# Where the last three batches' softmax steps stand: eb6 behind gp7, pd6 behind pe7, later pL5 and pe5, batch 4's maximum ahead of its clip

## The chip, the core and the metric

The kernel runs on one core of a Trainium2 chip. Its engines work side by side, each in the order of its own list: TensorE (PE) multiplies, VectorE (DVE), ScalarE (ACT) and GpSimd (POOL) work element by element, SyncE (SP) issues DMA transfers, and ScalarE issues some too. The metric is the time of one execution on the device, in microseconds; less is better.

## What is computed

```python
X = np.fft.rfft(x, axis=1)                       # x: 8 batches x 2496 x 256
Yr = Xr @ w_r - Xi @ w_i + b_r
Yi = Xr @ w_i + Xi @ w_r + b_i
Y = softshrink(Yr, 0.01) + 1j * softshrink(Yi, 0.01)
x = np.fft.irfft(Y, n=2496, axis=1).reshape(19968, 256)

logits = x @ phi                                 # phi: 256 x 32
d = exp(logits - logits.max(0)); d /= d.sum(0) + 1e-9
slot_input = d.T @ x                             # 32 slots, 4 for each of 8 experts
slot_out[e] = relu(slot_input[e] @ w1[e]) @ w2[e]
c = exp(logits - logits.max(1)); c /= c.sum(1) + 1e-9
out = c @ slot_out
```

The softmax `d` runs over all 19968 tokens, so its maximum and its sum are carried from batch to batch; the softmax `c` runs over the 32 slots of each token.

## The kernel before

A transform of length 2496 = 39 x 64 is done in two stages by matrix products. Each batch has five steps of four frequencies (`NGRP` = 5). In a step PE makes `px` (second stage), `pk` and `py` (the product with the weights, each operand split into a high and a low part), the other engines make `xth`, `xtl`, `xsm`, `xs` (operands) and `ut`, `rt` (softshrink), and PE makes `pq` (logits in the frequency domain, copied as `lg`). `pt` are transposes of `rt` into `T`.

When a batch's five steps are through, its softmax chain follows (`c_stages(b)`, for the last batch `last_chain`), interleaved with the steps of the next batches. Its pieces, with the batch number behind the name:

- `pg`: inverse of the 64-point stage; `g_sb` is written to DRAM as `gd` (320 KB) and read back transposed as `gp` (four loads, 330 KB together). In the last chain the write is cut in three (192, 64 and 64 KB) and issued by ScalarE.
- `pL`: logits, in two halves `pL_0`, `pL_1`. DVE reduces each half to a maximum `mx`, ScalarE copies it to `L`. In batches 0 to 5 `pL` has high and low parts (`chpL`, `clpL`) and both halves use the one buffer of the PSUM tag `ps`.
- `pm`, `mall`, `dg`, `pb`: running maximum, transposed and spread over the partitions.
- `ee`: exponential; `pe`: first stage of it (in batches 0 to 5 from `chpe`, `clpe`); `ea`, written to DRAM as `ed` and read back as `eb` (two loads, 320 KB together, in rows of 128 bytes).
- `pd`: second stage, `dd`; `pr`: the sum of `dd` times `T`; `acc`: running sum, updated from `pr` by `slots_out`.

After batch 7's `pr` come `psl` (slot inputs), `hps` and `po` (the two products of the experts, whose weights `w` were loaded on the way), `prep`, and the output: `pc` (transposes of `c`), `pq`, `ost` and 41 writes.

The order on every engine is set by the program's own order. Each piece is a generator that yields a time in planned microseconds; a heap runs whichever comes first, and what is recorded then is issued in that order. The numbers are in `PLAN`: `late` has one list for each of the batches 4, 5 and 6 (`pL`, `pe`, `pd`, `pr` are offsets from the batch's start `t0`), `T_` the numbers of the last part, whose origin is `TB`. In `last_chain`, transposes wait in `fills` under a key and `fill(...)` lets them go where PE would otherwise wait; (2, 0) to (4, 1) are batch 6's, (7, 0) belongs to batch 7's first step. `halves` runs one product in two halves: it yields, issues the matmuls, yields `de` later and lets the result be copied (`evac`). All matmuls are recorded in line 244, transposes in 641, elementwise operations in 183, SyncE's DMAs in 238, ScalarE's in 241.

Of the kernel before, what the change touches and what calls it, by code (L numbers as in the profile page):

```python
# [17 lines left out]
B, N, D = 8, 2496, 256  # L18
# [34 lines left out]
def _constants():  # L53
# [133 lines left out]
def fourier_soft_moe_kernel(ctx: ExitStack, tc: tile.TileContext, t: dict, out: bass.AP):  # L187
# [19 lines left out]
    def psum(tag, name):  # L207
        return pp.tile([128, 512], F32, tag=tag, name=name, bufs=psum_bufs[tag])
# [8 lines left out]
    x = t["x"]  # L217
# [6 lines left out]
    V, A, P = (_InOrder(tc, e) for e in (nc.vector, nc.scalar, nc.gpsimd))  # L224
# [12 lines left out]
    def sp(**kw):  # L237
        tc.keep_in_program_order(nc.sync.dma_start(**kw))
# [4 lines left out]
    def mm(**kw):  # L243
        tc.keep_in_program_order(nc.tensor.matmul(**kw))  # L244
# [61 lines left out]
    xs = wtile([128, 6 * KS], F32R, "xs", "xs")  # L306
# [9 lines left out]
    ident, sgn, suni, sinv, dsc, dmask = (cols[k] for k in ("ident", "sgn", "suni", "sinv", "dsc", "dmask"))  # L316
    f1, m2 = cols["f1"][:P1], cols["m2"][:Q1]
# [369 lines left out]
        else:  # L687
            cins[b] = [cb[:, :GX, :], cb[:, GX:, :]]

    def halves(n, t0, times, out, const, fr, src, evac, de=0.25):  # L690
        xs = []
        xw = 352 if n in ("m2", "f1") else 320
        low = lambda x, xh, xl: V.tensor_tensor(out=xl, in0=x, in1=xh.bitcast(F32), op=ALU.subtract)
        late = n == "m2"
        for h in range(2 * fr[n]):
            dh = (PLAN["clm"] if late else PLAN["cl"][1]) * h
            yield t0 + times[0] - PLAN["cl"][0] + dh
            x = src(h)
            m, w = x.shape[0], x.shape[1] * x.shape[2]
            xh, xl = (  # L700
                wtile([128, 352], F32R, z, f"{z}{out[0]}_{h}")[:m, :w].rearrange("p (k s) -> p k s", s=S)
                for z in ("ch", "cl")
            )
            A.copy(out=xh, in_=x)
            xs.append((xh, xl))
            yield t0 + times[0] - PLAN["cl"][0] + dh + PLAN["cl"][2]
            low(x, xh, xl)
        for h in range(2):
            yield t0 + times[h]
            ps = psum("pl" if n == "suni" and h and not fr[n] else "ps", f"{out[0]}_{h}")  # L710
            if fr[n]:
                ch, cl = const_hl[n]
                for i, (w_, x_) in enumerate(((ch, xs[h][0]), (cl, xs[h][0]), (ch, xs[h][1]))):
                    mm(out=out[1](ps)[:, :xw], lhsT=w_, rhs=x_, start=i == 0, stop=i == 2)
            else:
                mm(out=out[1](ps)[:, :xw], lhsT=const, rhs=src(h), start=True, stop=True)
            yield t0 + times[h] + de
            evac(h, out[1](ps))

    def c_stages(b):  # L720
        ct_ = "ps"
        K_ = dict(PLAN, **PLAN["late"].get(str(b), {}))
        t0 = 20 * b + 20 + LAG
# [3 lines left out]
        fr = K_["fr"]  # L727
# [10 lines left out]
        for r in range(R):  # L738
# [14 lines left out]
        def logits_out(h, ps):  # L753
# [19 lines left out]
        ps = psum(ct_, f"pm{b}")  # L773
# [11 lines left out]
        else:  # L785
# [3 lines left out]
        ps = psum(ct_, f"pb{b}")  # L789
# [4 lines left out]
            out=ee, in0=L, in1=ps[:P1, :32].unsqueeze(1).broadcast_to([P1, G, S]), op=ALU.subtract  # L794
# [11 lines left out]
        yield t0 + K_["pe"][1] + 0.35  # L806
        ed = dr.tile([2 * K1, NP, S], F32, tag="ed", name=f"ed{b}")
        sp(out=ed.rearrange("k (r g) s -> (k r) g s", r=R), in_=ea)
        yield t0 + K_["pe"][1] + 0.9
        eb = wtile([128, K1, S], F32, "gp", f"eb{b}")  # L810
        for c in range(2):
            sp(out=eb[c * 64 : c * 64 + 64], in_=ed[c * K1 : c * K1 + K1, :N2].rearrange("k n s -> n k s"))
# [5 lines left out]
                out=dd[:, h * 10 : h * 10 + 10, :],  # L818
# [13 lines left out]

    prs = {}
# [181 lines left out]
    T_ = PLAN["T_"]  # L1015
# [5 lines left out]
    def last_chain():  # L1021
        b = B - 1
        for (k0, k1), tk in zip(((0, 12), (12, 16), (16, 20)), T_["pg"]):
            ks = slice(k0, k1)
            n = (k1 - k0) * S
# [4 lines left out]
            ps = psum("pf", f"pg{b}_{k0}")  # L1030
# [5 lines left out]
        for r in range(R):  # L1036
# [67 lines left out]
        eb = wtile([128, K1, S], F32, "gp", f"eb{b}")  # L1104
# [183 lines left out]
    for j in range(NBLK):  # L1288
# [81 lines left out]
```

## Time and profile before

| | |
|---|---|
| median of 3 runs | 523.17 us (522.37 to 523.2) |
| profiled execution | 522.57 us |
| its span | 520.8 us |
| PE busy | 502.7 us (97%) |
| DVE, ACT, POOL busy | 405.6, 312.8, 295.5 us |
| granted PE clock, mean | 0.993 |

A row of a timeline gives the start, the duration, the engine, the source line and the operation with its output and input; in brackets stands how long the engine was idle before it, and what released it. Neighbouring matmuls overlap: one is listed with some 0.28 us, and the next starts 0.12 us after it, so for PE the step from start to start counts. A clock of 1.00 is 2.4 GHz. Engines other than PE have idle time nearly everywhere, and it costs nothing unless PE waits for them.

### The profile page before, as it was taken

Reading aid. Unit: us, or ns where it says so; the run is one execution under the profiler, and the core shown is the slowest. Engines: PE = TensorE matmul, PEld = TensorE weight load, DVE = VectorE, ACT = ScalarE, POOL = GpSimd, SP = SyncE. Lnnn points to the kernel's source line nnn. Section 1 sums busy time; section 2 is a strip of 40 time slices with the busy share of each in tenths; the row PEclk is TensorE's granted clock in tenths of the full one; section 3 lists DMA queues with packets and bytes.
Section 4 is the critical chain, followed back from the end, with each engine's and each line's share of the span. In section 5 each row is a group of like instructions: output and inputs, shape, how many; then the busy total and the mean of one; then the engine's idle time right before and its main releaser. Section 6 shows DMA issues by size and latency. Waiting matters only on the chain.

```text
span 520.8 us, 12050 instructions
## 1 busy us (share of the span) xinstructions
PE 502.7 (97%) x4473; PEld 440.9 (85%) x4473; DVE 405.6 (78%) x778; ACT 312.8 (60%) x704; POOL 295.5 (57%) x278
## 2 busy tenths in 40 slices
PE   8999999999999999999999999999999999999991
PEld 7888899999899999999998998889899877458880
DVE  3796787799968898889888988897798856257771
ACT  2776576768676766676667666654543436148761
POOL 1486687768676757675767577776466303054210
PEclk9999999999999999999999999999999999999997
DMA  8555456665765657565756576676655577979998
GB/s 295 220 185 185 136 183 227 168 238 130 280 166 188 162 200 210 174 162 193 210 176 164 188 212 211 165 274 209 235 143 158 180 174 213 409 249 406 400 409 333
DMA packets 90146, 114.85 MB, mean 221 GB/s; under 512 B 46478, under 2 KB 65868, under 8 KB 90088
## 3 DMA queue, kind: packets, MB, share of 16 engines
q1 hardware_dynamic: 89377, 112.90, 66.0%
q10 hardware_dynamic: 711, 1.19, 0.7%
q8 instruction: 35, 0.57, 0.4%
q14 instruction: 23, 0.19, 0.1%
HBM read 66.72 MB, written 47.34 MB: 219 GB/s over the span
## 4 chain that ended last, share of the span: by engine, by line
PE 85%; DVE 5%; DMA 4%; ACT 2%; issue 1%; SPq 1%; DVEq 0%; ACTq 0%
PE py L244 20%; PE px L244 13%; PE pk L244 10%; PE pq L244 10%; PE pa L244 9%; PE pt L641 6%; PE pr L244 3%; PE pe L244 2%; PE q L244 2%; PE pc L1169 2%; PE pL L244 2%; PE pg L244 1%; PE hps L244 1%; PE po L244 1%; DMA gp<-gd 1%; DMA out<-ost 1%
## 5 line engine op out<-in xcount | busy, mean ns | idle before, releaser
L183 POOL TENSOR_TENSOR xs<-xsm,xs 128x256 fp32r<-128x256 f32 x77 | 63.2, 821 | 97.7 <-DVE xs L183 67.5
L183 POOL TENSOR_TENSOR rt<-ut,rt 128x512 f32<-128x512 f32 x79 | 105.0, 1329 | 14.8 <-DVE rt L183 13.4
L183 POOL TENSOR_TENSOR xl<-xr,xh 117x512 fp32r<-117x512 f32 x72 | 97.7, 1358 | 15.2 <-ACT xh L183 15.2
L244 PE MATMUL px<-smov,ap 128*128 128x128 f32 x640 | 85.1, 276 | 0.4 <-DVE ap L183 0.3
L244 PEld LDWEIGHTS px<-smov,ap 128*128 128x128 f32 x640 | 80.3, 191 | 5.1 <-DVE ap L183 0.6
L183 DVE SCALAR_TENSOR_TENSOR ut<-py,pk,k 128x256 f32<-128x256 f32 x160 | 69.5, 475 | 11.4 <-PE py L244 11.1
L183 ACT CAST xth<-px 128x512 fp32r<-128x512 f32 x80 | 46.9, 587 | 45.4 <-PE px L244 23.2
L183 ACT COPY ast<-pa 128x512 f32<-128x512 f32 x75 | 44.2, 590 | 45.7 <-PE pa L244 45.7
L183 DVE TENSOR_TENSOR xtl<-px,xth 128x512 fp32r<-128x512 f32 x80 | 54.7, 684 | 20.3 <-ACT xsm L183 20.3
L244 PE MATMUL pk<-xs,w_rh 128*128 128x256 f32 (+1 forms) x320 | 66.1, 290 | 0.0
L183 DVE TENSOR_SCALAR rt<-ut 128x512 f32<-128x512 f32 x69 | 63.8, 924 | 0.5
L244 PE MATMUL py<-xth,nwsh 128*128 128x256 f32 (+1 forms) x160 | 53.4, 334 | 0.1
L244 PEld LDWEIGHTS pk<-xs,w_rh 128*128 128x128 f32 x320 | 51.8, 189 | 0.6 <-DVE xs L183 0.3
L183 ACT CAST xh<-xr 117x512 fp32r<-117x512 f32 x75 | 47.5, 636 | 1.0 <-DMA xr<-in_x 1.0
L641 PE MATMUL pt<-pk,rt 128*128 128x128 f32 x320 | 45.2, 274 | 1.2 <-DVE ap L183 1.1
L183 ACT COPY T<-pt 128x512 f32<-128x512 f32 x67 | 39.8, 600 | 8.9 <-PE pt L641 7.3
L244 PE MATMUL py<-xth,wdh 128*128 128x256 f32 (+1 forms) x160 | 44.8, 280 | 0.0
L244 PE MATMUL py<-xtl,wdh 128*128 128x256 f32 (+1 forms) x160 | 44.6, 278 | 0.0
L244 PE MATMUL py<-xtl,nwsh 128*128 128x256 f32 (+1 forms) x160 | 44.5, 278 | 0.0
L244 PE MATMUL py<-xth,nwsl 128*128 128x256 f32 (+1 forms) x160 | 44.5, 278 | 0.0
L244 PE MATMUL py<-xth,wdl 128*128 128x256 f32 (+1 forms) x160 | 44.4, 278 | 0.0
L244 PE MATMUL pk<-xs,w_rl 128*128 128x256 f32 (+1 forms) x160 | 44.4, 278 | 0.0
(196 smaller groups left out, 1192.3 us busy)
## 6 DMA issues: line engine op xcount, KB each, us to landing
out<-ost SPq DMA_DIRECT2D x37, 512.0 KB
xr<-in_x SPq DMA_DIRECT2D x35, 512.0 KB
ap<-adr SPq DMA_DIRECT2D x70, 256.0 KB
adr<-ast SPq DMA_DIRECT2D x21, 768.0 KB
w<-in_moe_w SPq DMA_DIRECT2D x25, 512.0 KB
w<-in_moe_w SPq DMA_DIRECT2D x12, 256.0 KB
x<-in_x SPq DMA_DIRECT2D x11, 256.0 KB
eb<-ed SPq DMA_DIRECT2D x16, 160.0 KB
```

The source lines that it names most:

```text
L183: return lambda *a, **k: self.tc.keep_in_program_order(f(*a, **k))
L244: tc.keep_in_program_order(nc.tensor.matmul(**kw))
L641: tc.keep_in_program_order(nc.tensor.transpose(out=out, in_=in_, identity=identity))
L1169: nc.tensor.transpose(out=pc[:, i * P1 : (i + 1) * P1], in_=chls[b][x][:, 2 * (r + i) : 2 * (r + i) + 2].rearrange("p g h s -> p (g h s)") ...
```

## The change

No arithmetic is added or removed; every instruction of before is still there. What moves:

- Batch 6's `eb` loads are planned at 21.015 instead of 0.9 behind `pe`, and stand on SyncE's list behind the four `gp7` loads.
- Batch 6's `pd` is planned at 30.6 instead of 20.25, and stands behind `pe7`; its two halves use the tags `pl` and `pf` (`pt` in the list), and its results are read at once.
- The second half of batch 7's first transposes (`pt7_0_1`) becomes a filler, key (7, 1), and stands ahead of `pe7`; step 1 of batch 7 (`pt7_1`) moves ahead of `pr6`.
- The last three transposes `pc0_8` of batch 0's `c` stand behind `pd7`.
- Batch 5: `pL` from 6.5, 7.2 to 7.02, 8.05 and `pe` from 11.35, 12.35 to 12.05, 12.6.
- Batch 4: the first half's `evac` 0.05 behind its matmuls instead of 0.25, which puts its maximum ahead of the clip `rt`.
- `slots_out` of batches 0 to 4 is 0.65 behind the last `pr` instead of 0.2: `acc` stands behind the next `xtl`, `xsm`, `xs` on DVE.

```diff
-'6': {... 'pd': [20.25, 20.62], ...}
+'6': {... 'eb': 21.015, 'pt': ['pl', 'pf'], 'de': 0.005, 'pd': [30.6, 30.61], ...}
-'5': {... 'pL': [6.5, 7.2], ... 'pe': [11.35, 12.35], ...}
+'5': {... 'pL': [7.02, 8.05], ... 'pe': [12.05, 12.6], ...}
+'4': {'me': [0.05, 0.25], ...}
...
-            ps = psum("pl" if n == "suni" and h and not fr[n] else "ps", f"{out[0]}_{h}")
+            ps = psum(tags[h] if tags else "ps", f"{out[0]}_{h}")
...
-            yield t0 + times[h] + de
+            yield t0 + times[h] + de[h]
...
-        yield t0 + K_["pe"][1] + 0.9
+        yield t0 + K_.get("eb", K_["pe"][1] + 0.9)
...
-        yield tk + (0.01 if b >= B - 3 else 0.2)
+        yield tk + (0.01 if b >= B - 3 else 0.65)
         slots_out(b)
...
-            key = (g_, h) if b_ == B - 2 and g_ >= 2 else (7, 0) if (b_, g_, h) == (B - 1, 0, 0) else None
+            key = (g_, h) if b_ == B - 2 and g_ >= 2 else (7, h) if (b_, g_) == (B - 1, 0) else None
...
-        fill((4, 1), (7, 0))
+        fill((4, 1), (7, 0), (7, 1))
...
+    at(10.9, fill, (7, 1))
...
-    for t_, f_, *a_ in ((T_["cl"], c_load, 0), (11.9, c_prep, 0), *((12.45 + 0.01 * i, c_trans, 0, i, V if i == 4 else A) for i in (0, 4, 8))):
+    for t_, f_, *a_ in ((T_["cl"], c_load, 0), (11.9, c_prep, 0), *((t_, c_trans, 0, i, V if i == 4 else A) for t_, i in ((12.45, 0), (12.49, 4), (19.5, 8)))):
```

SyncE's list at the start of the last chain, before (`ed6` is the write that `eb6` reads back, `w14` are expert weights, `cin0` is batch 0's `c`):

```order
L238 DMA ed6_6240<-ea6_6161 120x704
L238 DMA w14_0_6242<-in_moe_w1 128x512
L238 DMA w14_1_6243<-in_moe_w1 128x512
L238 DMA eb6_6256<-ed6_6240 64x20x32 x2
L238 DMA gp7_6412<-gd7_6263 40x22x32 x2
L238 DMA gp7_6412<-gd7_6263 40x20x32
L238 DMA gp7_6412<-gd7_6263 40x2x32
L238 DMA cin0_6419<-c_dr0_131 117x512
```

The two `eb6` loads are issued there ahead of `gp7`. SyncE's list at the same place now:

```order
L238 DMA ed6_6240<-ea6_6161 120x704
L238 DMA w14_0_6242<-in_moe_w1 128x512
L238 DMA w14_1_6243<-in_moe_w1 128x512
L238 DMA gp7_6402<-gd7_6259 40x22x32 x2
L238 DMA gp7_6402<-gd7_6259 40x20x32
L238 DMA gp7_6402<-gd7_6259 40x2x32
L238 DMA eb6_6409<-ed6_6240 64x20x32 x2
L238 DMA cin0_6413<-c_dr0_131 117x512
```

The two `eb6` loads have moved behind the four `gp7` loads and stand right ahead of `cin0`.

PE's list at the end of `pr5`, some way ahead of `pL7`, before (`pk0` holds the identity matrix):

```order
L244 MATMUL pr5_6355<-T5_3_5520,dd5_5714 32x256 x4
L244 MATMUL pr5_6355<-T5_4_5521,dd5_5714 32x256 x4
L244 MATMUL pd6_0_6380<-eb6_6256,pk1_120 128x320
L641 MATMUL pt6_0_0_6384<-pk0_119,rt6_0_0_5079 128x128
L641 MATMUL pt6_0_0_6384<-pk0_119,rt6_0_1_5151 128x128
```

`pd6_0` stands right behind `pr5` there, and `pd6_1` eight transposes further on. PE's list around `pe7` now:

```order
L641 MATMUL pt7_0_1_6482<-pk0_119,rt7_0_0_5774 128x128
L641 MATMUL pt7_0_1_6482<-pk0_119,rt7_0_1_5822 128x128
L244 MATMUL pe7_0_6496<-ee7_6487,pk1_120 120x352
L244 MATMUL pe7_1_6499<-ee7_6487,pk1_120 120x352
L244 MATMUL pd6_0_6511<-eb6_6409,pk1_120 128x320
L244 MATMUL pd6_1_6514<-eb6_6409,pk1_120 128x320
L641 MATMUL pt7_1_0_6519<-pk0_119,rt7_1_0_5874 128x128
```

Both halves of `pd6` have left the transposes ahead of `pL7` and stand behind `pe7`, and the four transposes of `pt7_0_1` stand ahead of it.

DVE's list around batch 5's maximum, before:

```order
L183 TENSOR_SCALAR rt6_2_1_5437<-ut6_2_1_5434 128x512
L183 TENSOR_REDUCE mx5_5355<-pL5_0_5471 117x32
L183 TENSOR_TENSOR xtl6_4_0_5467<-px6_4_0_5447,xth6_4_0_5466 128x512
L183 TENSOR_TENSOR xsm6_4_0_5468<-px6_4_0_5447,xsm6_4_0_5468 128x256
L183 CAST xs_118<-xsm6_4_0_5468 128x256
L183 TENSOR_REDUCE mx5_5355<-pL5_1_5498 117x32
L183 SCALAR_TENSOR_TENSOR ut6_3_0_5509<-py6_3_0_5480,pk0_119,k16_3_5478 128x4x64 x2
L183 TENSOR_REDUCE mall_126<-pm5_5507 128x1
```

Each reduction `mx5` is done there as soon as its half of `pL5` is. DVE's list at the same place now:

```order
L183 TENSOR_SCALAR rt6_2_1_5437<-ut6_2_1_5434 128x512
L183 TENSOR_TENSOR xtl6_4_0_5466<-px6_4_0_5440,xth6_4_0_5465 128x512
L183 TENSOR_TENSOR xsm6_4_0_5467<-px6_4_0_5440,xsm6_4_0_5467 128x256
L183 CAST xs_118<-xsm6_4_0_5467 128x256
L183 TENSOR_REDUCE mx5_5355<-pL5_0_5488 117x32
L183 SCALAR_TENSOR_TENSOR ut6_3_0_5498<-py6_3_0_5474,pk0_119,k16_3_5472 128x4x64 x2
L183 TENSOR_REDUCE mx5_5355<-pL5_1_5516 117x32
L183 TENSOR_REDUCE mall_126<-pm5_5525 128x1
```

The first reduction `mx5` from `pL5_0` has moved behind `xtl6_4_0`, `xsm6_4_0` and `xs`, and the second behind `ut6_3_0`.

## Rows read from the trace of the kernel before

**Rows 1.** Page, part 4, whole span: chain that ended last, by engine.

```profile
PE 85%; DVE 5%; DMA 4%; ACT 2%; issue 1%; SPq 1%; DVEq 0%; ACTq 0%
```

**Rows 2.** Timeline (start us, us, engine, operation [idle before]), batch 4's maximum: DVE, then PE.

```profile
312.40 0.41 DVE L183 TENSOR_SCALAR rt<-ut 128x512 f32<-128x512 f32 x1
...
312.84 0.28 PE L244 MATMUL py<-xtl,wdh 128*128 128x256 f32 x1
...
313.30 0.42 PE L244 MATMUL pL<-chpL,m2h 120*117 120x352 f32 x1 [0.18 <-DVE mx L183]
```

**Rows 3.** Timeline, batch 5's maximum: PE, then DVE.

```profile
360.36 0.32 PE L244 MATMUL pL<-chpL,m2l 120*117 120x352 f32 x1
360.82 0.42 PE L244 MATMUL pL<-clpL,m2h 120*117 120x352 f32 x1
...
361.13 0.42 DVE L183 TENSOR_SCALAR rt<-ut 128x512 f32<-128x512 f32 x1
...
362.21 0.68 DVE L183 TENSOR_TENSOR xtl<-px,xth 128x512 fp32r<-128x512 f32 x1
...
363.46 0.55 DVE L183 TENSOR_REDUCE mx<-pL 117x32 f32<-117x384 f32 x1
```

**Rows 4.** Timeline, batch 5's exponential: GpSimd, DVE, PE.

```profile
370.09 1.29 POOL L183 TENSOR_TENSOR rt<-ut,rt 128x512 f32<-128x512 f32 x1 [0.36 <-DVE rt L183]
...
370.57 1.19 DVE L183 TENSOR_TENSOR clpe<-ee,chpe 117x352 fp32r<-117x352 f32 x1 [0.56 <-ACT chpe L183]
...
372.94 0.52 DVE L183 TENSOR_TENSOR clpe<-ee,chpe 117x352 fp32r<-117x352 f32 x1
...
370.95 0.32 PE L244 MATMUL pe<-chpe,f1l 117*120 117x352 f32 x1
371.82 0.42 PE L244 MATMUL pe<-clpe,f1h 117*120 117x352 f32 x1 [0.55 <-DVE clpe L183]
```

**Rows 5.** Timeline of SyncE's queue, last chain: issue times of loads.

```profile
417.69 2.22 SPq L238 DMA_DIRECT2D eb<-ed  x2
...
423.37 2.71 SPq L238 DMA_DIRECT2D gp<-gd  x4
...
438.00 1.42 SPq L238 DMA_DIRECT2D eb<-ed  x2
```

**Rows 6.** Chain in order of time (start us, us, what): two writes of gd.

```profile
301.96 2.41 DMA gd<-g_sb
...
420.16 3.19 DMA gd<-g_sb
```

**Rows 7.** Windows: engines' busy us, PEclk, DMA share, GB/s, in the last chain.

```profile
419.50:422.00 2.50, 2.47 (x23) 2.23 (x21) 2.26 (x4) 1.48 (x4) 0.00 (x0) 1.00 0.90 164
424.60:427.00 2.40, 2.40 (x19) 1.95 (x16) 1.67 (x3) 0.58 (x1) 0.00 (x0) 1.00 0.81 127
427.60:434.00 6.40, 5.87 (x40) 4.71 (x39) 5.05 (x12) 3.66 (x9) 0.00 (x0) 1.00 0.79 283
436.80:442.50 5.70, 5.41 (x47) 4.94 (x47) 4.58 (x7) 3.84 (x8) 4.93 (x9) 1.00 0.91 219
```

**Rows 8.** Timeline of PE in the last chain.

```profile
426.06 0.70 PE L244 MATMUL pd<-eb,pk 128*128 128x320 f32 x2
426.61 1.06 PE L641 MATMUL pt<-pk,rt 128*128 128x128 f32 x8
...
427.90 1.41 PE L244 MATMUL pL<-gp,pk 120*117 120x352 f32 x4 [0.23 <-DMA gp<-gd]
...
431.60 1.07 PE L641 MATMUL pt<-pk,rt 128*128 128x128 f32 x8
...
432.97 1.45 PE L244 MATMUL pe<-ee,pk 117*120 117x352 f32 x4 [0.30 <-ACT ee L183]
...
440.69 1.02 PE L1169 MATMUL pc<-pk,chl 117*128 117x117 f32 x8
...
442.56 1.32 PE L244 MATMUL pd<-eb,pk 128*128 128x320 f32 x4
```

More of the change, by code (lines that the diff above doesn't have):

```diff
@@ L152 @@
     "to": 0.7,
-    "late": {'6': {'cms': [11.5, 19.69, 854.1, 854.2, 854.2, 854.2], 'pd': [20.25, 20.62], 'pr': [31.55, 31.6, 31.65, 31.7, 31.75], 'pL': [6.05, 6.5], 'pm': 8.05, 'mo': 0.1, 'pb': 9.05, 'eo': 0.4, 'pe': [11.1, 11.5], 'pg': [0.875, 1.275], 'fr': {'sinv': 0, 'm2': 0, 'f1': 0, 'suni': 0}}, '5': {'cms': [14.3, 14.8, 15.6, 20.0, 20.8, 21.5], 'pg': [1.1, 1.8], 'pL': [6.5, 7.2], 'pm': 8.52, 'de': 0.68, 'mo': 0.1, 'pb': 9.05, 'eo': 0.1, 'fr': {'sinv': 1, 'm2': 1, 'f1': 1, 'suni': 0}, 'pe': [11.35, 12.35], 'pd': [18.9, 19.3], 'pr': [40.2, 40.21, 40.22, 40.23, 40.24]}, '4': {'pr': [18.4, 20.49, 24.49, 28.49, 32.49]}},
@@ L154 @@
-    "T_": {'wl': [[-45, 'r'], [-44, 'r'], [-43, 'r'], [-31.0, 't'], [-30.7, 't'], [-29.4, 't'], [-27.6, 't'], [-27.8, 't'], [-11, 'a'], [-10.3, 'a'], [-9.6, 'a'], [-9.45, 'sm'], [-9.4, 'xs'], [-8.3, 'x'], [-8.1, 'x'], [1.06, 'x'], [1.07, 'h'], [1.08, 'h'], [13.55, 'h'], [13.55, 'h'], [13.55, 'h'], [13.55, 'h'], [13.55, 'h'], [13.61, 't'], [13.61, 't'], [13.61, 't'], [13.61, 't'], [13.61, 't'], [13.7, 'T'], [13.7, 'T'], [13.7, 'T']], 'cl': 1.02, 'cp': 46.5, 'ct': 46.6, 'du': [[-4.5, 0], [-2.4, 0], [1.2, 0]], 'd1': [5, 2, 4, 0, 0, 0], 'cm': [19.9, 19.91, 19.92, 25, 25.1, 25.2], 'cm7': [0.1, 0.12, 0.3, 0.4, 1, 1], 'ye': 0.2, 'te': [[5.6, 0.2], [5.5, 0.4]], 'pg': [-7, -3.25, -0.35], 'yt': 0.5, 'wr': -30.6, 'tp': [0, 0.9, 1.05, 0.3], 'tt': [[-3.6, -0.3, -0.25, -0.2, -6.5], [0.6, 0.7, 0, 0, 0], [12, 12.1, 12.2, 12.3, 12.4]], 'tg': {(5, 4): ('ps', 'pl'), (5, 0): ('pl', 'ps')}, 'eg': {(5, 4, 1): 'A', (6, 2, 1): 'A', (6, 4, 0): 'V', (6, 4, 1): 'A'}, 'z': 13.55, 'th': [0.1, 0.12], 'tl': [0.2, 0.25]},
+    "late": {'6': {'cms': [11.5, 19.69, 854.1, 854.2, 854.2, 854.2], 'eb': 21.015, 'pt': ['pl', 'pf'], 'de': 0.005, 'pd': [30.6, 30.61], 'pr': [31.55, 31.6, 31.65, 31.7, 31.75], 'pL': [6.05, 6.5], 'pm': 8.05, 'mo': 0.1, 'pb': 9.05, 'eo': 0.4, 'pe': [11.1, 11.5], 'pg': [0.875, 1.275], 'fr': {'sinv': 0, 'm2': 0, 'f1': 0, 'suni': 0}}, '5': {'cms': [14.3, 14.8, 15.6, 20.0, 20.8, 21.5], 'pg': [1.1, 1.8], 'pL': [7.02, 8.05], 'pm': 8.52, 'de': 0.68, 'mo': 0.1, 'pb': 9.05, 'eo': 0.1, 'fr': {'sinv': 1, 'm2': 1, 'f1': 1, 'suni': 0}, 'pe': [12.05, 12.6], 'pd': [18.9, 19.3], 'pr': [40.2, 40.21, 40.22, 40.23, 40.24]}, '4': {'me': [0.05, 0.25], 'pr': [18.4, 20.49, 24.49, 28.49, 32.49]}},
@@ new lines @@
+    "T_": {'wl': [[-45, 'r'], [-44, 'r'], [-43, 'r'], [-31.0, 't'], [-30.7, 't'], [-29.4, 't'], [-27.6, 't'], [-27.8, 't'], [-11, 'a'], [-10.3, 'a'], [-9.6, 'a'], [-9.45, 'sm'], [-9.4, 'xs'], [-8.3, 'x'], [-8.1, 'x'], [1.06, 'x'], [1.07, 'h'], [1.08, 'h'], [13.55, 'h'], [13.55, 'h'], [13.55, 'h'], [13.55, 'h'], [13.55, 'h'], [13.61, 't'], [13.61, 't'], [13.61, 't'], [13.61, 't'], [13.61, 't'], [13.7, 'T'], [13.7, 'T'], [13.7, 'T']], 'cl': 1.02, 'cp': 46.5, 'ct': 46.6, 'du': [[-4.5, 0], [-2.4, 0], [1.2, 0]], 'd1': [5, 2, 4, 0, 0, 0], 'cm': [19.9, 19.91, 19.92, 25, 25.1, 25.2], 'cm7': [0.1, 0.12, 0.3, 0.4, 1, 1], 'ye': 0.2, 'te': [[5.6, 0.2], [5.5, 0.4]], 'pg': [-7, -3.25, -0.35], 'yt': 0.5, 'wr': -30.6, 'tp': [0, 0.9, 1.05, 0.3], 'tt': [[-3.6, -0.3, -0.25, -0.2, -6.5], [0.6, 0.7, 0, 0, 0], [12, 11.45, 12.2, 12.3, 12.4]], 'tg': {(7, 0): ('pt', 'ps'), (5, 4): ('ps', 'pl'), (5, 0): ('pl', 'ps')}, 'eg': {(5, 4, 1): 'A', (6, 2, 1): 'A', (6, 4, 0): 'V', (6, 4, 1): 'A'}, 'z': 13.55, 'th': [0.1, 0.12], 'tl': [0.2, 0.25]},
@@ L688, in c_comb, with halves @@
             cins[b] = [cb[:, :GX, :], cb[:, GX:, :]]
-    def halves(n, t0, times, out, const, fr, src, evac, de=0.25):
+    def halves(n, t0, times, out, const, fr, src, evac, de=(0.25, 0.25), tags=None):
         xs = []
@@ L767, in c_stages @@
             logits_out,
+            K_.get("me", [0.25] * 2),
         )
@@ L822, in c_stages @@
             ),
-            K_.get("de", 0.25),
+            [K_.get("de", 0.25)] * 2,
+            K_.get("pt", None if fr["suni"] else ("ps", "pl")),
         )
```

## The prediction

> **What bounds the kernel now.** I read the chain of waits first: TensorE (PE) holds 85% of the span, so a microsecond counts only if a wait on PE goes away [rows 1]. Then I read PE's timeline for places where the step from one start to the next is longer than the same step elsewhere. Between 60 and 420 us there are few, and this change touches two of them: batch 4's maximum at 313 us [rows 2], and batch 5's maximum and exponential at 361 and 371 us [rows 3, 4]. The rest is the last chain, from 424 us on [rows 8]; there DMA round trips stand between PE's pieces [rows 5 to 7]. After the last `pr` the kernel runs on from what that chain gives it (slots, two matrix products, output), and none of that is edited, so I carry a shift there to the end one to one.
>
> **Batch 4: maximum ahead of clip.** VectorE (DVE) did a clip (0.41 us from 312.40) before the reduction that frees `pL4`'s only PSUM buffer; PE's next `pL` started 0.46 us after the `py` ahead of it, where such a step is 0.12, and it waited for that reduction [rows 2]. With the reduction first, it ends some 0.4 us sooner and the wait is gone: 0.34 of the step, and a little of the slow first `pL` (0.42 us): **0.4 us gained** (bounds 0 and 0.45). The clip is late by half a microsecond for a subtraction that nobody waits for here.
>
> **Batches 0 to 4: the accumulator update moves behind three operations.** Order on DVE only; I find no PE wait there that it ends, except beside batch 5's exponential, counted below. Zero.
>
> **Batch 5: pL behind the next py, pe behind the next px.** Before, PE lost 0.30 us inside `pL5_0`: the step from 360.36 to 360.82 is 0.46 us, where 352 columns at the 0.12 of 256 make 0.16 [rows 3]. Now a whole `py` (1.4 us) stands ahead, so that wait goes. But `pL5_1` now follows after one `px` (0.8 us), and its buffer is free only after the first reduction, which DVE does behind the trio `xtl`, `xsm`, `xs`. The trio starts when the clip ends (361.13 + 0.42 = 361.55) and lasts 1.25 us (362.21 to 363.46) [rows 3]; a reduction of 0.5 follows, to 363.3. PE gets there at 360.2 (`pL5_0`'s begin before, a step ahead of 360.36) + 1.4 + 0.5 + 0.8 = 362.9. So a new wait of 0.4 to 0.5 takes the place of the old: **0.1 lost**, and up to 0.5 if ScalarE, which then copies the second half, the maxima and the next `xth` in a row, brings `dg` late for `pb`. The exponential: PE's step from 370.95 to 371.82 is 0.87 us, 0.7 too long, for `clpe`, which took 1.19 us because it ran beside a GpSimd subtraction until 371.38; the other `clpe` took 0.52 [rows 4]. Now `clpe` comes behind the trio, at 372.0 to 372.5, while PE, with `px` first, is ready for it at about 372.1. A wait of 0.4 to 0.5 stays where 0.7 was: **0.2 gained** (bounds: 0.7, if `clpe` is in time, and 0.6 lost, if GpSimd's next subtraction is first and holds it for 0.7 as before). Batch 5 together: zero, from 0.6 gained to 1.1 lost.
>
> **The last chain up to pL7.** SyncE loaded `eb6` from 417.69 to 419.91, in packets so small that the 16 DMA engines were 0.90 busy with 164 GB/s until 422 [rows 5, 7]. ScalarE's last write of `gd7` went out at 420.16 in the middle of it and landed 3.19 us later; the same tensor of an earlier batch, all 320 KB at once, landed in 2.41 [rows 6], and this piece is 64 KB. With `eb6` behind `gp7` the write is alone. I take 2.0 us for it (under 2.41, the nearest row, since a fifth of the bytes move; 3.19 if nothing changes): 1.2 us sooner, bounds 0 and 1.45, past which PE is not ready for `pL7`. SyncE then issues `gp7` (four loads from 423.37 [rows 5]) 1.2 us sooner, unhindered as now; `eb6` follows in the same queue and does not overtake it. PE must be ready by then: `pd6`, two matmul groups of 0.55 (426.06 to 426.61) to 0.7 us each (its listed time), is gone from there, so the last transposes (426.61, 1.06 us) end at 426.4 and not 427.7 [rows 8]. `pL7` starts at 426.7 instead of 427.90.
>
> **From pL7 to pe7.** 5.07 us (427.90 to 432.97), a chain through DVE, PE and ScalarE with PE's fillers measured to it [rows 8]. The four transposes of `pt7_0_1` that move ahead of `pe7` take half of 0.9 us (431.60, eight of them) and fit in the 0.47 us that PE stood idle for `ee` [rows 8]. No change in length: `pe7` at 431.8.
>
> **From pe7 to pd7.** Before, 9.59 us (432.97 to 442.56). Out go 0.45 for `pt7_0_1` and the third group of `pc0`: eight transposes from 440.69 end at 441.6, so `pc0_8` with its wait took 0.97. In comes `pd6`, 1.2. That makes 9.4, so PE is at `pd7` at 441.2, and 0.2 goes back because `pc0_8` now stands between `pd7` and `pr7`, where PE waited for DVE only in part. `pr6` waits for `dd6`, but 0.9 us of `pt7_1` lie between, enough for DVE's 0.5 us a half. The other condition is `eb7`: its loads were issued at 438.00 for 1.42 us [rows 5], and `pd7` shows that it was there by 442.56; 1.2 sooner that is 441.3 at the latest, so it may cost 0.1. **The last chain gains 1.1 us**, bounds 0 (`gd7` as late as before) and 1.5.
>
> **Sum.** 0.4 + 0 + 1.1 = 1.5 us. The profiled execution took 522.57 us (span 520.8 and 1.77 around it): 521.07. The median of the three runs, 523.17, lies 0.6 above the profiled one, and comparisons go by it: **521.7 us**.
>
> **Rivals.**
> (a) `gd7` lands no sooner: its 3.19 us are mostly fixed time after the last byte. Against it speaks the 2.41 us row [rows 6], for it that the write is small and still slow. Then PE waits 1.5 us ahead of `pL7`, and only the fillers gain: 0.4 of batch 4 and nothing else. 522.8.
> (b) `eb7` becomes the bound. `eb6`, some 320 KB at the 127 GB/s of `gp7` [rows 7], is 2.4 us of DMA work that now stands ahead of `cin` and four weight loads; these kept the engines 0.79 busy from 427.6 to 434.0 [rows 7] and would end at 434.0 - 1.2 + 2.4 = 435.2. `ed7`, whose write starts near 434.5 now, runs into 0.7 us of them; if it waits for all, `eb7` and `pd7` are that much later and 0.4 + 0.4 remain. 522.4. The Trainium skill bears on this: "DMA: Bandwidth & Descriptors", section "Queues, rings and completion order", says that a DMA's completion signal is ordered behind the earlier writes of its DMA engine, whichever queue they came from. By that, the late `gd7` [rows 6] agrees with a write held by `eb6`, and `ed7` would be held in the same way by the weights.
> (c) Batch 5 loses its bad bounds, 1.1 us (0.5 at `pb`, 0.6 at `clpe`), as worked out above. 522.8.
> (d) Slower: the clock. Without `pd6`, PE has only transposes between `pr5` and `pL7` and then an idle gap of up to 1.5 us. If the granted clock falls from 2.4 to 1.2 GHz there, the 5.07 us to `pe7`, nearly all PE work, last up to 4.6 longer: 526.3. It decides by the granted clock of the stretch behind `pL7`. Against it: over the 5.7 us of transposes from 436.8 to 442.5, with waits in them, the clock read 1.00 [rows 7]. The Trainium skill, "TensorE: Matmul & The Clock Gate", section "Why this matters for your kernels", warns of idle gaps between bursts of matmuls for this reason; the trace shows none that cost the clock here.
>
> **How the numbers follow.** Forecast 0.50, (a) 0.18, (b) 0.13, (c) 0.13, (d) 0.06. Under the forecast the gain lies between 0.9 and 2.5, so almost all of it is faster by over 0.2% (1.05 us, about what a measurement of this kernel tells from no change). (a) to (c) are within 0.2%, save some of (b) that is faster, and (c) with (a) that comes near the other side. Faster 0.53, same 0.38, slower 0.09. Range: the low end is every good bound, 0.45 + 0.6 + 1.5 = 2.55 below 523.17, 520.6; the high end is (a) and (c) together, 0.4 gained and 1.1 lost, and nothing in the last chain: 523.9, drawn in to 523.5, since both at once are unlikely.
>
> **What would show it.** Right: `gd7` landing within 2.4 us of its last issue, `pL7` some 1.2 us sooner against `pr5`'s end than now less `pd6`, no wait on PE ahead of `pe7`, `pL4_1` without a wait. Wrong: PE idle for a microsecond or more ahead of `pL7` (a); PE idle ahead of `pd7` and released by `eb7` (b); `pL5_1` or `pe5_0` with waits over 0.6 us (c); a granted clock under 1.00 behind 426 us (d).

## The result, and the profile after

The changed kernel took **526.03 us** (median of 6 runs, 525.46 to 526.74). The kernel before took 523.18 us beside it (6 runs, 522.37 to 523.81). The ratio is 1.0062, with a 95% interval of 1.0051 to 1.0074: slower by 0.6%, where the prediction had 0.3% faster and a high end of 523.5. The profiled span is 523.9 us, 3.1 longer than before.

To see where, I laid TensorE's rows of the two traces side by side and took the differences in start time at ten instructions which both kernels have. The table shows them for every kernel of this study (the Experiments say what each is; a row is read from one profiled execution): how many us later than in the kernel before TensorE begins the instruction in the head of the column (its start before stands there; pm1 is the transpose for batch 1's maximum, and so on). The first column is mostly a shift from the loads at the start. What counts is how a row changes from column to column.

| kernel | pm1 162.95 | pm2 214.83 | pm3 266.71 | pg4 298.35 | pL4_1 313.30 | pe4_1 326.18 | pg5 349.22 | pm6 404.94 | pe7 432.97 | slots 446.82 |
|---|---|---|---|---|---|---|---|---|---|---|
| after | 0.11 | 1.33 | 2.56 | 3.78 | 3.44 | 3.72 | 3.66 | 4.45 | 3.19 | 3.22 |
| e1_acc_back | 0.21 | 0.21 | 0.20 | 0.19 | -0.16 | 0.14 | 0.15 | 0.75 | -0.69 | 0.34 |
| e2_acc_alone | 0.19 | 1.42 | 2.65 | 3.86 | 3.85 | 3.85 | 3.78 | 4.07 | 3.86 | 3.78 |
| e3_batch5_back | 0.30 | 0.30 | 0.30 | 0.30 | -0.03 | 0.29 | 0.30 | 0.15 | -1.26 | -0.59 |
| e4_last_chain_alone | 0.42 | 0.42 | 0.41 | 0.39 | 0.38 | 0.38 | 0.39 | 0.30 | -1.06 | -0.69 |
| m1_acc_behind_p_sb | 0.56 | 0.56 | 0.55 | 0.53 | 0.19 | 0.50 | 0.99 | 1.80 | 0.21 | 0.36 |
| m2_acc_behind_ut | -0.28 | 0.94 | 2.17 | 3.38 | 3.06 | 3.38 | 3.31 | 4.12 | 2.55 | 3.52 |
| m3_no_small_addition | -0.35 | -0.23 | -0.06 | 0.10 | -0.24 | 0.07 | -0.32 | 0.25 | -1.16 | -0.78 |
| m4_weight_behind_eb7 | 0.88 | 0.87 | 0.96 | 0.96 | 0.64 | 0.94 | 0.95 | 0.81 | -0.60 | 0.43 |
| m5_split_subtraction | 0.51 | 1.19 | 1.87 | 2.55 | 2.21 | 2.52 | 2.14 | 2.74 | 1.50 | 2.01 |
| b5_pL_alone | 0.43 | 0.42 | 0.42 | 0.42 | 0.09 | 0.40 | 0.41 | 0.71 | -0.37 | 0.05 |
| b5_pe_alone | 0.17 | 0.17 | 0.16 | 0.15 | -0.17 | 0.12 | 0.14 | 0.39 | -1.15 | -0.48 |
| x1_clip_behind_clpe | 0.29 | 0.29 | 0.29 | 0.28 | -0.05 | 0.26 | 0.27 | -0.34 | -1.53 | -0.91 |

The row of the changed kernel says it at once: three steps of 1.22 to 1.23 us by 298 us, where I had expected nothing; a gain of 0.34 at batch 4's maximum that is gone again by 326; 0.79 lost from pg5 to pm6, most of it in batch 5; 1.26 gained in the last chain.

The first of the three steps, in the changed kernel's timeline (start us, us, engine, operation, [idle before]): VectorE (DVE), then GpSimd (POOL), then TensorE (PE).

```profile
185.72 0.42 DVE L183 COPY acc<-pr 128x257 f32<-128x257 f32 x1
...
187.23 0.88 DVE L183 TENSOR_REDUCE cs<-cb 117x22 f32<-117x704 f32 x1
188.14 1.07 DVE L183 TENSOR_SCALAR cs<-cs 117x22 f32<-117x22 f32 x1
189.25 0.29 DVE L183 RECIPROCAL cs<-cs 117x22 f32<-117x22 f32 x1
189.46 0.23 DVE L183 TENSOR_TENSOR p_sb<-pq,pk 128x128 f32<-128x128 f32 x1
...
187.90 1.28 POOL L183 TENSOR_TENSOR xl<-xr,xh 117x512 fp32r<-117x512 f32 x1
...
188.39 0.27 PE L244 MATMUL pk<-xs,w_rh 128*128 128x256 f32 x1
189.74 0.66 PE L641 MATMUL pt<-pk,rt 128*128 128x128 f32 x4 [1.08 <-DVE p_sb L183]
```

The same place in the kernel before:

```profile
187.71 0.18 DVE L183 TENSOR_SCALAR cs<-cs 117x22 f32<-117x22 f32 x1
...
188.13 0.23 DVE L183 TENSOR_TENSOR p_sb<-pq,pk 128x128 f32<-128x128 f32 x1
188.27 1.09 DVE L183 TENSOR_SCALAR rt<-ut 128x512 f32<-128x512 f32 x1
...
187.79 1.29 POOL L183 TENSOR_TENSOR xl<-xr,xh 117x512 fp32r<-117x512 f32 x1
...
188.41 0.66 PE L641 MATMUL pt<-pk,rt 128*128 128x128 f32 x4
```

The accumulator update `acc` takes 0.42 us and now stands ahead of `ut`, `dd` and the sum `cs`. Before, the small addition on `cs` (22 numbers in each of 117 partitions, 0.18 us) began at 187.71, just ahead of GpSimd's subtraction for `xl`. Now it begins at 188.14, behind it, and takes 1.07 us: it ends, at 189.21, just behind that subtraction (187.90 + 1.28 = 189.18). `p_sb` is late by 1.3 us, and TensorE needs its PSUM buffer for `pt`. Before, the subtraction held something too, the clip `rt` behind `p_sb` (1.09 us, 0.41 in [rows 2]), for which nobody waited. The other two steps look the same, at 241 and 294 us. By form and place, the addition reads so (count, min/median/max ns, first and last start), before and after:

```profile
L183 DVE TENSOR_SCALAR cs<-cs x8: 178/178/661, 135.1 to 461.5; 117x22 f32<-117x22 f32 x8
```

```profile
L183 DVE TENSOR_SCALAR cs<-cs x8: 178/830/1071, 135.2 to 464.7; 117x22 f32<-117x22 f32 x8
```

The one long addition of before (0.66 us) starts at 459 us and ends 0.03 us behind a GpSimd subtraction too; it is there after as well.

Batch 5 after, where [rows 3, 4] show it before: DVE and PE.

```profile
366.16 0.55 DVE L183 CAST xs<-xsm 128x256 fp32r<-128x256 f32 x1
366.63 0.51 DVE L183 TENSOR_REDUCE mx<-pL 117x32 f32<-117x352 f32 x1
...
365.73 1.06 PE L244 MATMUL px<-smov,ap 128*128 128x128 f32 x8
367.19 0.42 PE L244 MATMUL pL<-chpL,m2h 120*117 120x352 f32 x1 [0.41 <-DVE mx L183]
...
376.19 0.32 PE L244 MATMUL pe<-chpe,f1l 117*120 117x352 f32 x1
376.88 0.43 PE L244 MATMUL pe<-clpe,f1h 117*120 117x352 f32 x1 [0.37 <-DVE clpe L183]
```

`pL5_1` waits 0.41 us for the reduction, as worked out, and `pe5_0` still waits for `clpe`.

The last chain after, where [rows 5, 8] show it before: the queues of ScalarE and SyncE, then PE.

```profile
424.62 0.33 ACTq L241 DMA_DIRECT2D gd<-g_sb  x1
...
426.48 2.73 SPq L238 DMA_DIRECT2D gp<-gd  x4
429.25 1.40 SPq L238 DMA_DIRECT2D eb<-ed  x2
...
441.13 1.42 SPq L238 DMA_DIRECT2D eb<-ed  x2
...
431.08 1.41 PE L244 MATMUL pL<-gp,pk 120*117 120x352 f32 x4
...
436.16 1.44 PE L244 MATMUL pe<-ee,pk 117*120 117x352 f32 x4
...
445.59 1.31 PE L244 MATMUL pd<-eb,pk 128*128 128x320 f32 x4
```

`gd7`'s last write is issued at 424.62 and `gp7` goes out 1.86 us later, where the write alone took 3.19 us before [rows 6]. `pL7`, `pe7` and `pd7` start without a wait for data. The granted clock is 1.00 from 424 to 444 us.

### The profile page after: what moved, and what is told of

It is laid out like the page before. It is cut to its first block, busy times and chain, and to the rows that moved or that the text cites. A ratio compares the mean times of both kernels' runs of the same rounds, so it can differ in the third digit from the quotient of the medians.

```text
span 523.9 us, 12053 instructions
## 1 busy us (share of the span) xinstructions
PE 503.1 (96%) x4473; PEld 441.3 (84%) x4473; DVE 402.7 (77%) x778; ACT 313.1 (60%) x704; POOL 295.9 (56%) x278
## 3 DMA queue, kind: packets, MB, share of 16 engines
q10 hardware_dynamic: 711, 1.19, 0.7%
## 4 chain that ended last, share of the span: by engine, by line
PE 83%; DMA 6%; DVE 6%; ACT 2%; issue 1%; SPq 1%; DVEq 0%; ACTq 0%
PE py L244 21%; PE px L244 13%; PE pa L244 10%; PE pq L244 10%; PE pk L244 9%; PE pt L641 6%; DMA w<-in_moe_w 3%; PE pr L244 3%; PE q L244 2%; PE pe L244 2%; PE pL L244 2%; PE pg L244 2%; PE pc L1172 1%; DMA out<-ost 1%; DVE cs L183 1%
## 5 line engine op out<-in xcount | busy, mean ns | idle before, releaser
L183 DVE TENSOR_SCALAR rt<-ut 128x512 f32<-128x512 f32 x69 | 58.3, 845 | 0.5
```

The costliest lines, as they stand in the source:

```text
L183: return lambda *a, **k: self.tc.keep_in_program_order(f(*a, **k))
```

## Experiments

Theory H (held instruction): in some forms, a VectorE instruction that starts while a GpSimd instruction runs gets done only when that one has ended, and the order on VectorE decides which instruction this hits and whether TensorE waits for it. The rivals stand with each run. The times of a run are compared with the kernel before on the same chip: 523.11 us beside e1 to e4, 522.57 beside m1 to m4, 523.06 beside m5, the two halves of batch 5 and x1. Medians of this kernel scatter by about half a microsecond, so effects under 1 us are read from the rows, by the table above, and rest on one execution of each kernel.

**The accumulator update: undone, and alone.** Two kernels with one edit, forth and back:

```diff
-        yield tk + (0.01 if b >= B - 3 else 0.65)   # e1: the changed kernel, back
+        yield tk + (0.01 if b >= B - 3 else 0.2)
-        yield tk + (0.01 if b >= B - 3 else 0.2)    # e2: the kernel before, forth
+        yield tk + (0.01 if b >= B - 3 else 0.65)
```

> The changed kernel with the accumulator update of batches 0 to 4 back where it was (0.2 behind the last pr, not 0.65). Theory H (held instruction): in batches 0, 1 and 2 the late update pushes the small addition on cs into GpSimd's subtraction for xl, which holds it for 1.0 to 1.1 us, and TensorE then waits for p_sb; undone, 3 x 1.22 = 3.7 us come back: 522.4 (0.7 below the kernel before), cs at 0.18 us everywhere. Theory D (the update costs only its own 0.42 to 0.48 us of VectorE, three times): 1.3 us come back, 524.7. Theory L (the loss is in batch 5 and the last chain): no change, 526.

> The kernel before with nothing but the accumulator update of batches 0 to 4 moved from 0.2 to 0.65. Theory H: 3.7 us slower, 526.8, with three waits of 1.1 us on TensorE ahead of pt near 188, 241 and 294 us. Theory D: 1.3 us slower, 524.5. Theory L: no change, 523.2.

Measured: e1 522.95 us, ratio 1.0005 (0.9991 to 1.0019); e2 526.36 us, ratio 1.0062 (1.0048 to 1.0075). The one edit makes the loss: alone it costs 3.25 us in the median, where the whole change lost 2.85, and 3.67 us in the rows by 298 us; undone, the three steps are gone. Theories D and L fall; D's push is part of the cost, as m3 and m5 show below. That e1 ends near the kernel before, and not 0.7 below it, comes behind 430 us (the experiment on `eb7` below).

**Where the update stands, not how late it is.** Two kernels move it later still, to 1.6 (behind `p_sb`) and 1.2 (behind `ut`, ahead of `dd` and `cs`), in the line above.

> The changed kernel with the accumulator update of batches 0 to 4 not earlier but later still: 1.6 behind the last pr, where VectorE has done cs and p_sb. Theory H (only what stands ahead of the small addition on cs matters): the addition is back at 0.18 us, the three waits of 1.1 us ahead of pt are gone, 3.3 to 3.7 us come back, 522.5. Rival T (a late accumulator update costs by itself, the later the more): no better than the changed kernel, 526 or more.

> The changed kernel with the accumulator update one place later only: behind ut, still ahead of dd and cs. Theory H: the addition on cs begins as late as in the changed kernel, behind the begin of GpSimd's subtraction, and is held as there; 526 as the changed kernel. Rival U (the loss comes from ut, which the update delays by 0.42 us, and from GpSimd's work on ut): ut is early again, 522.5.

Measured: m1 522.92 us, ratio 1.0009 (0.9996 to 1.0021); m2 526.7 us, ratio 1.0069 (1.0046 to 1.0093). The latest place costs nothing up to 326 us, the middle one costs 3 x 1.22 us although `ut` is early there. VectorE in m2:

```profile
186.11 0.42 DVE L183 COPY acc<-pr 128x257 f32<-128x257 f32 x1
...
187.75 1.07 DVE L183 TENSOR_SCALAR cs<-cs 117x22 f32<-117x22 f32 x1
```

Theories T and U fall. m1 pays elsewhere: batch 4's `pr` uses the same PSUM buffer and waits 0.82 us for the update of batch 3 (the step from 0.50 to 0.99 in the table).

**What is held.** One kernel without the addition, one with GpSimd's subtraction in two halves:

```diff
-        V.tensor_scalar(out=cs, in0=cs, scalar1=1e-9, scalar2=None, op0=ALU.add)   # m3
...
+            if g == 14:                                                            # m5
+                copy(eh, xh, xs)
+                for i in range(GP):
+                    el.tensor_tensor(out=xl[:, i], in0=xs[:, i], in1=xh[:, i].bitcast(F32), op=ALU.subtract)
```

> The changed kernel without the addition of 1e-9 to cs (117x22), which is left out of the computation in all batches; the reciprocal follows the reduction directly. Theory H1 (any VectorE instruction that reads and writes SBUF is held by the running GpSimd operation): the reciprocal takes the hold, about 1.0 to 1.1 us instead of 0.29, and the loss stays: 525.5 to 526. Theory H2 (only some forms are held, the reciprocal not): reciprocal at 0.29, p_sb 1 us sooner, 3.3 us come back, 522.5.

> The changed kernel with GpSimd's subtraction for xl that the addition on cs runs into (117x512, 1.28 us) cut into two of 117x256 (about 0.7 us each), in every batch from the third on. If the addition waits for the end of the GpSimd instruction that is running: it ends with the first half, about 0.45 us instead of 1.07, and the wait ahead of pt falls from 1.1 to about 0.5 us, in the three places; 524.2. If it waits until GpSimd has nothing queued: 1.07 us or more, as the changed kernel, 526.

Measured: m3 522.53 us, ratio 1.000 (0.9976 to 1.0025); m5, a single run, 524.34 us. VectorE and GpSimd in m3 at the first of the three places:

```profile
187.69 0.29 DVE L183 RECIPROCAL cs<-cs 117x22 f32<-117x22 f32 x1
187.89 0.23 DVE L183 TENSOR_TENSOR p_sb<-pq,pk 128x128 f32<-128x128 f32 x1
188.04 0.98 DVE L183 TENSOR_SCALAR rt<-ut 128x512 f32<-128x512 f32 x1
...
187.45 1.29 POOL L183 TENSOR_TENSOR xl<-xr,xh 117x512 fp32r<-117x512 f32 x1
```

The reciprocal starts 0.24 us into the subtraction and takes its usual 0.29: it is not held, nor is `p_sb`, which reads PSUM. The next clip is, at no cost. H2 holds. VectorE, GpSimd and TensorE in m5:

```profile
188.54 0.54 DVE L183 TENSOR_SCALAR cs<-cs 117x22 f32<-117x22 f32 x1
...
188.29 1.44 POOL L183 TENSOR_TENSOR xl<-xr,xh 117x256 fp32r<-117x256 f32 x2
...
189.60 0.66 PE L647 MATMUL pt<-pk,rt 128*128 128x128 f32 x4 [0.54 <-DVE p_sb L183]
```

The addition ends at 189.08, about where the first half does (188.29 and half of 1.44 us: 189.01), and takes 0.54 us instead of 1.07. The three steps shrink to 0.68 us each (0.51, 1.19, 1.87, 2.55 in the table). So it waits for the end of the running instruction, not for an empty GpSimd.

The two kernels also split a step of 1.22 us into hold and push. m3 has no hold, but it saves the addition's own 0.21 us (187.71 to 187.92 in the kernel before) as well; its steps of 0.12 to 0.17 us and these 0.21 make 0.33 to 0.38 us for the push of `p_sb` alone, an estimate. The rest, nearly 0.9 us, is the hold (1.07 - 0.18). m5 agrees: 0.68 less its hold of 0.36 (0.54 - 0.18) is 0.32.

The trace of the kernel before is full of holds already: 102 VectorE instructions in it take over 0.08 us longer than the shortest of their form, and every one of them ends behind a GpSimd instruction by its own shortest time less 0.12 to 0.15 us: the clip (0.41 us alone) by 0.28, the cast (0.29) by 0.15, `clpe` (0.52) by 0.38, the addition (0.18) by 0.03. Of these 49 are the clip `rt`, 24 the cast `xs`, 28 differences of two tensors in SBUF, one the addition.

**Batch 5, and its two halves.** e3 is e1 with batch 5's numbers back; the other two put one of them late again:

```diff
-'5': {... 'pL': [7.02, 8.05], ... 'pe': [12.05, 12.6], ...}
+'5': {... 'pL': [6.5, 7.2], ... 'pe': [11.35, 12.35], ...}
```

> The kernel of e1_acc_back with batch 5's pL and pe back where they were as well, so that the maximum of batch 4 and the last chain are all that is left of the change. If batch 5 loses 1.1 us, as a comparison of the two traces by rows says: 1.1 below e1_acc_back, 521.4, and 1.7 to 1.8 below the kernel before. If batch 5 came out even, as the prediction had it: the same as e1_acc_back.

> The kernel of e3_batch5_back with batch 5's pL late (as in the change) and its pe where it was. Row comparison of the changed kernel: pL5 late loses 0.6 us up to pb, by the wait of pL5_1 for the reduction (0.41) and by pb coming 0.1 later; so 0.5 to 0.6 above e3_batch5_back. The prediction had 0.1 lost. If pL and pe only lose together: no more than 0.2.

> The kernel of e3_batch5_back with batch 5's pe late (as in the change) and its pL where it was. Row comparison: 0.3 to 0.5 us above e3_batch5_back, from chpe and clpe of the first half, both later than TensorE is ready for them. The prediction had 0.2 gained: 0.2 below.

Measured: e3 522.53 us, ratio 0.9993 (0.9981 to 1.0004); `pL` alone late 522.54 us, 0.9984 (0.9966 to 1.0003); `pe` alone late 522.18 us, 0.9981 (0.9964 to 0.9998). The medians cannot tell these apart, and the 1.1 us forecast between e1 and e3 came as 0.42. The rows can, at the `px` that starts at 376.30 us in the kernel before, where batch 5's exponential is through. From pg5 to there, against the kernel before, `pL` late has lost 0.44 us, `pe` late 0.28, both 0.72 (the same in e1 and in the changed kernel), and e3 nothing. Both halves lose and they add up. The column pm6 shows other numbers, because `pL6` at 400 us adds its own: from 376 us to pm6 e2, which has no edit of batch 5, loses 0.29, and e3 gains 0.14.

**The last chain alone, and what `eb7` waits for.** e4 is the kernel before with the edits of the last chain only. m4 is e3 with one weight load out of the way:

```diff
-        load_w("h", aq)
...
             sp(out=eb[c * 64 : c * 64 + 64], in_=ed[c * K1 : c * K1 + K1, :N2].rearrange("k n s -> n k s"))
+        load_w("h")
```

> The kernel before with the edits of the last chain alone (eb6 behind gp7, pd6 behind pe7, the other fillings). Theory H, with the sum of the parts: 1.25 us faster, 521.9, pL7 3.2 us or so behind where pr5 ends less pd6, and 0.4 slower than e3_batch5_back, which has the maximum of batch 4 too. If the parts do not add up (the last chain gains only because the stages ahead of it run late): within 0.4 us of the kernel before.

> The kernel of e3_batch5_back (batch 4's maximum and the last chain alone) with the 512 KB weight load that ScalarE issues behind ed7 moved behind eb7's loads on SyncE's queue. There pd7 waited 0.69 us for eb7. Theory W (the weight load, 0.67 us behind the write of ed7, takes DMA engines from ed7 and eb7): the wait goes, about 0.7 us sooner, 521.8. Rival F (ed7 and eb7 take their time whatever else moves): no change beyond 0.2 us, 522.5, pd7 still waits 0.5 us or more.

Measured: e4 522.10 us, ratio 0.9982 (0.9967 to 0.9998); m4 522.63 us, ratio 1.0002 (0.9988 to 1.0015), its `pd7` waits 1.06 us. In e4 the chain gains 1.36 us up to `pe7`, about as forecast, and gives back 0.37 behind it; that its median lies 0.4 below e3's and not above it is within the scatter. That is so in 11 of the 12 kernels with the new last chain: 1.1 to 1.6 us gained up to `pe7`, and then TensorE waits 0.17 to 1.06 us for `eb7` ahead of `pd7`. Only the profiled run of the changed kernel shows no such wait. Its two ends, PE's timeline of m1 and of e1:

```profile
442.73 1.32 PE L244 MATMUL pd<-eb,pk 128*128 128x320 f32 x4 [0.17 <-DMA eb<-ed]
```

```profile
442.71 1.32 PE L244 MATMUL pd<-eb,pk 128*128 128x320 f32 x4 [1.05 <-DMA eb<-ed]
```

From the issue of `ed7`'s write to the issue of `eb7`'s loads, which wait for it, pass 2.88 to 3.70 us; from there to `pd7`, where it waits, 4.38 to 5.31. TensorE is ready some 7.3 us behind the first issue, so the round trip is now as long as the work that hides it. Theory W falls, as far as this run tells: with the weight load away, TensorE's wait grew from 0.69 to 1.06 us, the write took longest of all (3.70) and the engines moved nothing for a while after it (windows of m4, engines' busy us, PEclk, DMA share, GB/s):

```profile
437.00:438.00 1.00, 1.00 (x24) 0.39 (x12) 0.00 (x0) 0.77 (x2) 0.41 (x1) 1.00 0.11 42
438.00:439.00 1.00, 1.00 (x13) 0.95 (x10) 0.48 (x1) 0.25 (x1) 1.00 (x2) 1.00 0.00 0
439.00:440.00 1.00, 1.00 (x12) 1.00 (x11) 0.69 (x1) 0.71 (x2) 1.00 (x3) 1.00 0.26 41
```

What makes the trip up to 0.9 us longer in one kernel than in another stays open. m4 moved a load that stands behind the write. Loads that SyncE had issued ahead of it still moved 0.21 MB in m4 while the write was out, and no run takes these away; their bytes alone do not set the trip, since in m1 they were 0.32 MB and the trip was the shortest of those with a wait.

**The hold as a lever.** If the hold is what costs, a place where it already cost before can be mended. In e3, as in [rows 4], GpSimd's subtraction holds `clpe_0` of batch 5. The clip that releases it goes one place back:

```diff
-        yield t0 + (PLAN["T_"]["th"][e] if end else PLAN["tho"])
+        yield t0 + (PLAN["T_"]["th"][e] if end else PLAN["tho"]) + 0.2 * ((b, grp, e) == (6, 3, 1))
```

> The kernel of e3_batch5_back with one instruction moved on VectorE: the clip that releases a GpSimd subtraction (rt, batch 6, group 3) goes behind clpe_0 of batch 5. There clpe_0 took 1.18 us, held by that subtraction, and TensorE lost 0.69 us inside pe5_0. If the hold is the cause: clpe_0 takes 0.52, the loss falls to 0.1 or less, and all behind is 0.6 us sooner: 521.9 where e3_batch5_back was 522.5. If clpe_0 is slow for another reason (its operands, ScalarE's copies beside it): 1.1 to 1.2 us as before, no gain.

Measured: 521.66 us, ratio 0.9974 (0.9958 to 0.9990), the best of the study and faster than both kernels. The hold is what made `clpe_0` slow. DVE, POOL and PE:

```profile
370.84 0.53 DVE L183 TENSOR_TENSOR clpe<-ee,chpe 117x352 fp32r<-117x352 f32 x1 [1.22 <-ACT chpe L183]
371.28 0.42 DVE L183 TENSOR_SCALAR rt<-ut 128x512 f32<-128x512 f32 x1
...
371.78 1.28 POOL L183 TENSOR_TENSOR rt<-ut,rt 128x512 f32<-128x512 f32 x1 [1.79 <-DVE rt L183]
...
371.22 0.32 PE L244 MATMUL pe<-chpe,f1l 117*120 117x352 f32 x1
371.42 0.42 PE L244 MATMUL pe<-clpe,f1h 117*120 117x352 f32 x1
```

`clpe_0` takes 0.53 us instead of 1.18, `pe5_0` has lost its wait, and all behind it begins 0.64 us sooner (-0.67 against -0.03 ahead of it, both against e3). Some 0.2 of that is lost again by pm6.

## Why the prediction was wrong, step by step

**The accumulator update: the step that failed.** The prediction costed it at zero, since it ended no wait of TensorE. It cost 3.67 us, more than everything else together. I had looked for what the move takes away and not for what it pushes: behind `acc` stand `ut`, `dd`, the sum, the addition, the reciprocal and `p_sb`, and for `p_sb` TensorE waits. The slack could be read before the run: the addition began 0.08 us ahead of GpSimd's subtraction (187.71, 187.79), and `p_sb` ended at 188.36 for a `pt` at 188.41. A push of 0.42 us was bound to run through both. Of each step of 1.22 us the push makes some 0.35, since `p_sb` had only 0.05 us to spare, and the hold nearly 0.9 (m3 and m5). I even had the hold, in `clpe`'s 1.19 us [rows 4], and took it for a feature of that one place; in the same trace 102 instructions show it. The Trainium skill has it as a rule: "SBUF — State Buffer", section "Who interferes with whom", says that VectorE and GpSimd share one pair of ports, which is locked for a whole instruction; that scalar operations, copies and casts on VectorE can ask for it, and operations with two SBUF inputs, while reductions never do; and that whichever comes first blocks the other. The traces agree in what is held (addition 1.07 us, clip 1.09, cast 0.55, `clpe` 1.19) and what is not (reduction 0.88, `p_sb` 0.23). That ports are the cause is the page's word; the runs show only which instructions are held and when they end.

**Batch 4's maximum.** Right at its place: `pL4_1` comes 0.32 to 0.35 us sooner against the columns around it in every kernel with the edit. Wrong behind it: at 326 us no more than 0.06 of it is left. "A subtraction that nobody waits for" leaves out what that subtraction holds, and VectorE's own list is no earlier by the swap. VectorE, GpSimd and TensorE in e3:

```profile
313.14 0.41 DVE L183 TENSOR_SCALAR rt<-ut 128x512 f32<-128x512 f32 x1
...
314.07 0.41 DVE L183 TENSOR_TENSOR xsm<-px,xsm 128x256 f32<-128x256 f32 x1
314.52 0.55 DVE L183 CAST xs<-xsm 128x256 fp32r<-128x256 f32 x1
...
313.63 1.29 POOL L183 TENSOR_TENSOR rt<-ut,rt 128x512 f32<-128x512 f32 x1 [1.23 <-DVE rt L183]
...
314.63 1.13 PE L244 MATMUL px<-smov,ap 128*128 128x128 f32 x8
```

TensorE gives back 0.14 us at the `px` at 314.63, which waits for `xsm` to end (314.07 + 0.41 = 314.48): reduction and clip changed places, so `xsm` behind both is no sooner. This is not the hold, which comes after it. The clip is later, so the subtraction runs until 314.92 and holds the cast for `xs`, which took 0.29 us before; what follows on VectorE comes 0.3 us later than the columns around it, ScalarE's copies behind the second maximum with it, and TensorE gives back another 0.16 us at 319.

**Batch 5.** Zero was the forecast, 1.1 lost its bad bound and rival (c); 0.72 came by 376 us, so (c) came in two thirds of its size. `pL`: the wait of 0.41 stood where I put it, but the trio ahead of the reduction took 1.5 us and not 1.25, because its cast was held (0.55); 0.24 were lost there and not 0.1, and 0.2 more at `pb` and `clpe`. `pe`: `clpe` was in time for GpSimd, and the step into it shrank from 0.85 to 0.68 as forecast, but ScalarE's cast `chpe` now comes behind `xth`, `xsm` and `k`. I had not looked at it. In b5_pe_alone the step from `px` to `pe5_0` is 1.05 us instead of 0.81, and 0.3 more are lost from `pe5_1` to the next `px`.

**The last chain.** Right in each step in the profiled run: `gp7` 1.86 us behind the write (taken: 2.0), `pL7` 1.26 sooner against its surroundings (1.2), 5.08 to `pe7` (5.07), 9.43 to `pd7` (9.4), 1.23 gained in all (1.1). Rivals (a) and (d) did not come; that the measured 526.03 us lies near (d)'s 526.3 is chance, for the granted clock was 1.00 there. Rival (b) did in the other kernels: `eb7` takes 0.2 to 1.1 us of the gain. The 0.1 that I allowed for it was too little; the cause that I gave, loads issued ahead of the write, is neither shown nor excluded by m4. (Its working has two slips that change little: 320 KB at 127 GB/s are 2.5 us, not 2.4, and no row gives 434.5 for `ed7`'s write, which was issued at 435.06 in the kernel before.) That the changed kernel's profiled run has no wait for `eb7` is luck, as the other 11 kernels show.

**The sum**, for the changed kernel: 0.11 at the start, 3.67 lost by the update, 0.06 gained in batch 4, 0.06 gained from 326 to 349 us, 0.72 lost in batch 5 and 0.07 ahead of pm6, 1.26 gained up to `pe7`, 0.03 lost behind it: 3.2 us later. (Between 326 and 349 us batch 3's update holds the addition for 1.00 us and costs 0.33; as much comes from a wait near 339 us that a late TensorE no longer has.)

## What to carry to other kernels

An instruction moved on VectorE is not free because nobody waits for it: list what stands behind it up to the first result that the bounding engine takes, and compare the slack there with its length. Where GpSimd works beside VectorE, look for instructions whose time in the trace is far above that of others of their form; small shifts decide which instruction is hit, and it pays to let the hold fall on one that nobody waits for (0.64 us in x1). A gain is worth only the slack of the next round trip behind it.

## What the runs showed of the hardware that I had not expected

An addition on 22 numbers a partition takes 0.18 us alone and up to 1.07 us beside GpSimd: how long it is held goes by when the other instruction ends, not by its own size, and it then ends behind that one by its own time less some 0.13 us (102 cases in the kernel before). A reciprocal on the same numbers is not held (0.29 us, 0.24 us into the same subtraction), so the form of an instruction matters and not only where its data lie. And a DRAM round trip of one tensor (`ed7` to `eb7`) took from 7.5 to 8.4 us up to its first user where that waited for it, and was as long in m4 (8.36), where the DMA engines stood almost idle for three of these us, as in e1 (8.35).
